# Operands of VectorE in PSUM, one scale per weight matrix, lo in one piece, and two evacuations by either engine

## The chip, the core and the metric

The kernel runs on one core of a Trainium2 chip. The core has a matrix engine (TensorE, PE in the views; its weight loads are the row PEld), VectorE (DVE), ScalarE (ACT), GpSimd (POOL) and SyncE (SP), which here only starts DMAs. The engines work side by side; each goes through its own queue in order and waits on semaphores for the others. SBUF is the memory of 128 partitions that all of them work in; PSUM holds eight banks of 512 fp32 columns, into which TensorE writes. The metric is the device time of one execution in microseconds. Inputs are laid out by the host before the launch and the output is put in order after it; neither is in the time.

## What is computed

Attention with normalised queries and keys (8 batches, 12 heads, 448 tokens, 64 columns a head), and behind it a two-layer block whose input is a mixture of each token with the one before:

```python
def rmsnorm(x, g):
    rms = np.sqrt(np.mean(x * x, axis=-1, keepdims=True) + 1e-06)
    return x / rms * g
q_n, k_n = (rmsnorm(q, g_q), rmsnorm(k, g_k))
scores = scale * np.matmul(q_n, k_n.transpose(0, 1, 3, 2))
scores = scores - np.max(scores, axis=-1, keepdims=True)
attn = np.exp(scores)
attn = attn / (np.sum(attn, axis=-1, keepdims=True) + 1e-09)
x = np.matmul(attn, v)            # heads side by side: 8 x 448 x 768
x_prev = x shifted by one token, the first one zero
xk = mu_k * x + (1.0 - mu_k) * x_prev
xr = mu_r * x + (1.0 - mu_r) * x_prev
k = np.maximum(xk @ w_k, 0.0)     # 768 x 1024
v = k * k @ w_v                   # 1024 x 768
r = 1.0 / (1.0 + np.exp(-(xr @ w_r)))   # 768 x 768
out = r * v
```

q, k and v are fp32; the three weight matrices come as 64-bit floats. Products are made in fp16 with each operand split in two, hi and lo (lo is what rounding to hi leaves over), as hi x hi + hi x lo + lo x hi, and for the first three quads in fp32.

## The kernel before

A *quad* is four heads of a batch (24 quads `u`), a *pair* is two of them (48). For each quad `stats` sums squares and takes the inverse root by three Newton steps on 28 columns (`rsqrt`, line 425; tiles `sst`, `stm`, `ss`), `preps` scales q and k and brings them into transposed form (`stk`). `scores` goes through seven *groups* a quad (168 in all): the products of 128 query rows with all keys, for two heads, into two PSUM banks. `expo` takes the row maximum (VectorE) and the exponential with its sum (ScalarE). `probs` and `split` divide by the sum and write hi (ScalarE) and lo (VectorE, two instructions: columns 384 to 447 first, then 0 to 383, into a tile `nat` in which lo is turned by 64 columns), which a DMA transpose carries to `pT`; 21 groups, those of the first three quads, go through `probs_pe` instead, with transposes on TensorE. `attends` multiplies a pair with v and ScalarE evacuates the result into `x`. `vprep` makes v's scale, hi (ScalarE) and lo (VectorE) for the pairs from 6 on.

`mix` makes xk and xr of a batch, twice six pieces of 448 columns: GpSimd scales the previous token into `df`, VectorE adds the scaled token, ScalarE writes hi and GpSimd lo. `moe` multiplies: first xk with w_k in eight pieces (`square`: ScalarE relu into `kf`, ScalarE square for hi, GpSimd square and lo), then for each 128 tokens xr with w_r and kk with w_v, by halves of 384 columns (`gate`: three ScalarE tanh of 128 columns with a scale each; `store`: VectorE product, GpSimd scaling by columns, DMA out).

The weights come in 20 tiles of 128 columns (8 of w_k, 6 of w_r, 6 of w_v), each in two halves. `wload` starts the DMAs on ScalarE's queue, in rows of 1 KB, into `raw`. `weights` makes fp32 of the 64-bit values (GpSimd the low bits, ScalarE the high ones into PSUM, VectorE puts them together in `wf`). `wsplit` makes a scale for each tile: the diagonal of its Gram matrix on TensorE, taken out with `dg`, summed over partitions, the maximum in `WSC`; then hi and lo, for tiles 1 to 13 by GpSimd scaling, ScalarE cast and GpSimd subtraction, for the others by ScalarE and VectorE. The first half of a batch in `moe` needs all of w_k, the second half needs all 20 tiles (`wdone == NW`).

The order of instructions on every engine is written out when the program is made: each of these functions is a thread that yields instructions, and `Plan.run` emits next the one that can start first by the planner's own clocks, with a bonus for priority. `price` says how long an operation takes, `held` models that VectorE and GpSimd block each other, `wprio` raises the weights' priority when they lag behind one tile per `W_GAP` (10 us). PSUM banks are handed out by `Share`: scores up to five and never the last free one, products (and the weights' high bits) two, `ot` two.

## Time and profile before

| | before |
|---|---|
| median of 3 runs (lowest, highest) | 1018.15 us (1014.79, 1019.3) |
| the profiled execution | 1015.21 us, span of its instructions 1013.4 us |
| granted TensorE clock, mean | 0.961 |
| TensorE busy | 926.0 us (91%) |
| VectorE busy | 812.7 us (80%) |
| ScalarE busy | 746.0 us (74%) |
| GpSimd busy | 691.8 us (68%) |
| DMA queue of SP (q1), of ScalarE (q10) | 129.20 MB, 57.0% of 16 engines; 17.77 MB, 5.9% |

The profile is one execution seen by the hardware profiler. Almost all instructions carry one line number, that of the planner's call, so groups are told apart by operation and tile names: `out<-in`, buffer numbers left out. Tile names ending in x (`natx`, `dfx`) are further buffers of the same kind, and some early tiles lie in space lent by `kk` and `xk` and carry that name. Busy time is the union of an engine's instructions; a busy TensorE need not be at its peak, as matmuls overlap.

### The profile page before, as it was taken

What the parts mean: (1) busy time and instruction counts of PE and PEld (TensorE: products, weight loads), DVE (VectorE), ACT (ScalarE), POOL (GpSimd) and SP (SyncE); (2) the same over time, 40 slices, a digit from 0 to 9 for tenths busy, and PEclk for the clock granted to TensorE, in tenths of its full rate; (3) what the DMA queues carried; (4) which work ended last, traced back from release to release, by engine and by line L of the source; (5) the groups of instructions that cost most, each with busy time, mean ns of one, the idle gap of its engine ahead of it and who ended that gap; (6) DMA issues with size and microseconds to landing.
All of it is one profiled execution on the core that took longest, in us unless ns stands there. A gap on an engine that the chain in (4) does not pass through costs nothing. (4 is left out here: it accounts for less than half of the span.)

```text
span 1013.4 us, 18593 instructions
## 1 busy us (share of the span) xinstructions
PE 926.0 (91%) x6082; PEld 485.8 (48%) x6082; DVE 812.7 (80%) x2260; ACT 746.0 (74%) x1756; POOL 691.8 (68%) x734
## 2 busy tenths in 40 slices
PE   2588869669999999999999999899999999999998
PEld 2354434335544555455545555355545454455564
DVE  5879998999998698979997998799997989763000
ACT  3667878878788789888887887878886988952311
POOL 2787889743798747877886859855987478556501
PEclk9878979869999999999999999999999999999999
DMA  7322349667788789569847977869858884640000
GB/s 248 119 80 86 118 120 221 170 166 169 172 165 168 143 197 203 133 152 201 207 105 173 214 158 161 161 131 201 175 126 177 186 183 110 146 107 32 1 32 32
DMA packets 371138, 148.17 MB, mean 146 GB/s; under 512 B 338272, under 2 KB 355168, under 8 KB 371040
## 3 DMA queue, kind: packets, MB, share of 16 engines
q1 hardware_dynamic: 351792, 129.20, 57.0%
q10 hardware_dynamic: 19248, 17.77, 5.9%
q8 instruction: 48, 0.79, 0.3%
q14 instruction: 50, 0.41, 0.1%
HBM read 51.98 MB, written 11.01 MB: 62 GB/s over the span
## 5 line engine op out<-in xcount | busy, mean ns | idle before, releaser
L273 PE MATMUL ps<-wvh,kk 128*128 128x384 f16 x896 | 233.1, 326 | 0.8 <-DVE nat L273 0.8
L273 ACT ACTIVATE ps<-ps,sums 128x448 f32<-128x448 f32 x294 | 181.9, 621 | 52.5 <-DVE sums L273 48.9
L273 PE MATMUL ps<-xk,wkh 128*128 128x448 f16 x768 | 210.5, 356 | 4.8 <-DVE wf L273 3.9
L273 DVE SCALAR_TENSOR_TENSOR nat<-ps,sums,nat 128x64 f16<-128x64 f32 x480 | 190.7, 439 | 19.2 <-ACT nat L273 17.8
L273 DVE TENSOR_REDUCE sums<-ps 128x1 f32<-128x448 f32 x336 | 193.7, 612 | 15.4 <-PE ps L273 15.1
L273 PE MATMUL ps<-wrh,xr 128*128 128x384 f16 x672 | 179.9, 331 | 2.1 <-DVE nat L273 2.0
L273 ACT ACTIVATE nat<-ps,sums 128x448 f16<-128x448 f32 (+1 forms) x272 | 167.8, 659 | 16.9 <-DVE sums L273 7.1
L273 PEld LDWEIGHTS <-kk 128*128 128x128 f16 (+1 forms) x1362 | 129.2, 98 | 98.7 <-issue 13.5
L273 PE MATMUL ps<-stk 64*128 64x448 f16 (+3 forms) x1104 | 134.2, 390 | 26.4 <-ACT xk L273 6.2
L273 PE MATMUL ps<-wvl,kk 128*128 128x384 f16 x448 | 146.0, 326 | 0.0
L273 PE MATMUL ps<-xk,wkl 128*128 128x448 f16 x384 | 136.5, 355 | 0.0
L273 PEld LDWEIGHTS <-xr 128*128 128x128 f16 x1008 | 96.4, 99 | 80.1 <-issue 16.9
L273 PE MATMUL ps<-wrl,xr 128*128 128x384 f16 x336 | 111.1, 331 | 0.0
L273 PEld LDWEIGHTS <-wkh 128*128 128x128 f16 x768 | 71.9, 99 | 81.6 <-issue 21.6
L273 POOL TENSOR_TENSOR o<-o,bsc 128x384 f32<-128x384 f32 x48 | 43.3, 902 | 88.3 <-DVE o L273 52.3
L273 DVE SCALAR_TENSOR_TENSOR o<-o,ps 128x384 f32<-128x384 f32 x56 | 30.5, 545 | 87.7 <-PE ps L273 59.2
L273 PE MATMUL ps<-pT,vh 128*64 128x448 f16 x588 | 93.8, 363 | 1.4 <-DMA pT<-nat 0.7
L273 ACT ACTIVATE o<-ps,bsc 128x128 f32<-128x128 f32 x144 | 45.6, 387 | 51.2 <-PE ps L273 33.1
L273 POOL TENSOR_TENSOR qk<-qk,ss 128x896 f32<-128x896 f32 x36 | 64.0, 1778 | 22.1 <-DVE ss L273 14.9
L273 PEld LDWEIGHTS <-stk 64*128 64x128 f16 x1008 | 35.0, 98 | 78.0 <-issue 35.5
L273 DVE SCALAR_TENSOR_TENSOR df<-x,bsc,df 128x448 f32<-128x448 f32 x68 | 61.0, 910 | 5.8 <-POOL df L273 5.7
L273 POOL TENSOR_TENSOR nat<-nat 128x448 f32<-128x448 f32 x41 | 48.2, 1175 | 23.6 <-ACT nat L273 17.1
(161 smaller groups left out, 1813.7 us busy)
## 6 DMA issues: line engine op xcount, KB each, us to landing
vf<-in_v_dram SPq DMA_DIRECT2D x48, 256.0 KB, 3.0
out_dram<-o SPq DMA_DIRECT2D x28, 384.0 KB, 2.7
...
```

What stands on the lines that cost most here:

```text
L273: r = op.fn(op.kw["out"], op.kw["value"]) if op.fn.__name__ == "memset" else op.fn(**op.kw)
```

## The change

- **VectorE's operands.** The Newton steps work with the sum and the helper in a PSUM bank; so do v's exponents. In `mix` ScalarE, no longer GpSimd, scales the previous token, into PSUM, and VectorE reads it there. v's hi and lo are made like the GpSimd tiles of the weights (GpSimd, ScalarE, GpSimd). Some small scalings (`probs_pe`, `batch_scales`, `outscale`) go to GpSimd. PSUM shares of their own: `wz` (2) for the weights' high bits, `pg` (1), `df` (2, not the last free bank).
- **lo.** `split` writes lo in one instruction of 448 columns, no longer turned; v comes from the host in 14 blocks in place of 8 (448 KB a pair from pair 6 on), with the rows that lo meets.
- **The weights' scales.** One scale per matrix. A tile is unpacked into the place of the next tile's hi and lo in `WS` (the last one into `wf`); the Gram matrices of all tiles add up in one bank `pg`; `wscale` makes the scale once, and then `wsplit` makes hi and lo tile by tile, each when the one before is done. The even tiles take the GpSimd way. `gate` becomes one tanh of 384 columns, `store` one GpSimd scaling of 768. The loads are started on SP's queue, from a layout in which a tile's half is contiguous in each partition.
- **Either engine.** The relu in `square` and the evacuation in `attends` go to ScalarE or VectorE, whichever the planner's clock has free first.
- **The planner.** New prices, `W_GAP` 7 us, one `wf`, two `df` throughout (before: a third one late).

The core of the diff (the removed lines of weights and wsplit, which stand in the listing above, are left out):

```diff
-WF_BUFS = 2
+WF_BUFS = 1
 PT_BUFS = 2
 STK_BUFS = 2
 X_BUFS = 9
 SC_SHARE = (5, 1)
 MM_SHARE = (2, 0)
 OT_SHARE = (2, 0)
-LOW_TILES = range(0, 20)
-POOL_TILES = range(1, 14)
+WZ_SHARE = (2, 0)
+PG_SHARE = (1, 0)
+DF_SHARE = (2, 1)
+POOL_TILES = range(0, 20, 2)
...
-W_GAP = 10e3
+W_GAP = 7e3
...
-LATE_BUFS = (("kf", 1), ("df", 1), ("nat", 1))
+LATE_BUFS = (("kf", 1), ("nat", 1))
...
+def shares(op):
+    aa = [x for x in op.kw.values() if isinstance(x, bass.AP)]
+    if op.eng == "POOL":
+        return True
+    if any(in_psum(x) for x in aa):
+        return False
+    return op.kw.get("in1") is not None or op.fn.__name__ in FAST
...
     def stats():
...
+            qs = yield from banks["df"].get()
+            sm, tm = qs[:, 0:NSS], qs[:, NSS:2 * NSS]
+            yield V.tensor_scalar(out=sm[:, 0:2 * NT], in0=ss[:, 0:2 * NT], scalar1=1.0 / HD, scalar2=1e-6, op0=ALU.mult, op1=ALU.add)
+            yield V.tensor_scalar(out=sm[:, 2 * NT:NSS], in0=ss[:, 2 * NT:NSS], scalar1=gm[:, 3:4], scalar2=gm[:, 4:5], op0=ALU.mult, op1=ALU.add)
+            yield from rsqrt(V, y, sm, tm)
+            banks["df"].put(qs)
...
     def vprep(js):
...
+            if V_POOL:
+                yield G_.tensor_scalar(out=vf, in0=vf, scalar1=sv, scalar2=0.0, op0=ALU.mult, op1=ALU.add)
+                yield A.copy(out=vh, in_=vf)
+                yield G_.tensor_tensor(out=vl, in0=vf[:, 0:2 * NSL], in1=vh[:, 0:2 * NSL], op=ALU.subtract)
...
     def split(j, sp, r, ph, E):
-        for a, n, o in ((S - HD, HD, S), (0, S - HD, S + HD)):
-            yield V.scalar_tensor_tensor(out=ph[:, j, o:o + n], in0=sp[:, a:a + n], scalar=r[:, j:j + 1], in1=ph[:, j, a:a + n], op0=ALU.mult, op1=ALU.subtract)
+        yield V.scalar_tensor_tensor(out=ph[:, j, S:2 * S], in0=sp[:, 0:S], scalar=r[:, j:j + 1], in1=ph[:, j, 0:S], op0=ALU.mult, op1=ALU.subtract)
...
     def attends():
...
-                yield A.activation(out=x[:, 1 + lo:1 + hi, :].rearrange("p t c -> p (t c)"), in_=av[:, o:o + (hi - lo) * HD], func=AF.Copy, scale=1.0 if iv is None else iv)
+                xo, ao = x[:, 1 + lo:1 + hi, :].rearrange("p t c -> p (t c)"), av[:, o:o + (hi - lo) * HD]
+                if plan.pick("ACT", "DVE") == "ACT":
+                    yield A.activation(out=xo, in_=ao, func=AF.Copy, scale=1.0 if iv is None else iv)
+                else:
+                    yield V.tensor_scalar(out=xo, in0=ao, scalar1=1.0 if iv is None else iv, scalar2=None, op0=ALU.mult)
...
     def mix(b, d, which, dst, df, cnt):
...
-        yield G_.tensor_scalar(out=df, in0=xp, scalar1=sc[:, j + ND:j + ND + 1], scalar2=0.0, op0=ALU.mult, op1=ALU.add)
-        yield V.scalar_tensor_tensor(out=df, in0=xc, scalar=sc[:, j:j + 1], in1=df, op0=ALU.mult, op1=ALU.add)
+        pb = yield from banks["df"].get()
+        yield A.activation(out=pb[:, 0:S], in_=xp, func=AF.Copy, scale=sc[:, j + ND:j + ND + 1])
+        yield V.scalar_tensor_tensor(out=df, in0=xc, scalar=sc[:, j:j + 1], in1=pb[:, 0:S], op0=ALU.mult, op1=ALU.add)
+        banks["df"].put(pb)
...
     def wload():
...
-                yield A.dma_start(out=raw[:, 0:hk, :], in_=w[i * P:(i + hk) * P, c * P:(c + 1) * P].bitcast(I32).rearrange("(i p) n -> p i n", p=P))
-                RAW[ci, i] = raw
+                yield SP.dma_start(out=raw[:, 0:2 * hk * P], in_=w[c, h].bitcast(I32))
+                RAW[ci, h] = raw
...
     def weights():
         for nm, w, kt, c, ci in WT:
+            if c == 0:
+                pg = yield from banks["pg"].get()
+            last = ci + 1 in (NF, NF + ND, NW)
+            nb = 2 if ci < NF else 1
+            if last:
+                wf = yield from R["wf"].get(ci < NF)
+                f = wf.rearrange("p i n -> p (i n)")[:, 0:kt * P]
+                WFT[nm] = wf
+            else:
+                f = WS[nm][:, c + 1].rearrange("p a i n -> p (a i n)").bitcast(F32)
             fi = f.bitcast(I32)
+            for h in range(2):
+                yield from until(lambda: (ci, h) in RAW and st["tq"] >= GATE_W)
+                raw = RAW.pop((ci, h))
+                n = kt * P // 2
+                cols = slice(h * n, (h + 1) * n)
+                zb = yield from banks["wz"].get()
+                z = zb[:, 0:n]
+                yield G_.tensor_scalar(out=fi[:, cols], in0=raw.bitcast(mybir.dt.uint8)[:, 0:8 * n].rearrange("p (n b) -> p n b", b=8)[:, :, 3], scalar1=-15.5, scalar2=2.0 ** -5, op0=ALU.add, op1=ALU.mult)
+                yield A.activation(out=z, in_=raw[:, 0:2 * n].rearrange("p (n two) -> p n two", two=2)[:, :, 1].bitcast(F32), func=AF.Prelu, scale=F64_EXP, alpha=F64_NEG)
+                yield V.scalar_tensor_tensor(out=fi[:, cols], in0=z.bitcast(I32), scalar=3, in1=fi[:, cols], op0=ALU.logical_shift_left, op1=ALU.bitwise_or)
+                banks["wz"].put(zb)
                 R["raw"].put(raw)
+            w16 = f.bitcast(BF16).rearrange("p (i n two) -> p i n two", two=2, n=P)[:, :, :, 1]
+            yield [T.matmul(form=("w", 110 * kt), out=pg[:, c % nb * P:(c % nb + 1) * P], lhsT=w16[:, i, :], rhs=w16[:, i, :], start=(c == 0 and i == 0), stop=(last and i == kt - 1)) for i in range(kt)]
+            if last:
+                plan.spawn(wscale(nm, kt, ci - c, ci + 1, pg, nb * P), wprio)
...
+    def wscale(nm, kt, c0, c1, pg, w):
+        sc = WSC[:, c0:c0 + 1]
         sci = sc.bitcast(I32)
+        dg = small.tile([P, 2 * P], F32, name="dg", bufs=1)[:, 0:w]
+        yield V.tensor_tensor(out=dg.rearrange("p (b n) -> p b n", n=P), in0=pg[:, 0:w].rearrange("p (b n) -> p b n", n=P), in1=bcast(ident[:, :], w // P), op=ALU.mult)
+        yield T.matmul(form=("f", 200 + 1.7 * w), out=pg[:, 0:w], lhsT=ones.broadcast_to([P, P]), rhs=dg, start=True, stop=True)
+        yield V.tensor_reduce(out=sc, in_=pg[:, 0:w], axis=AX.X, op=ALU.max)
+        banks["pg"].put(pg)
         yield V.tensor_scalar(out=sci, in0=sci, scalar1=24, scalar2=23, op0=ALU.logical_shift_right, op1=ALU.logical_shift_left)
         yield V.tensor_scalar(out=sci, in0=sci, scalar1=-1.0, scalar2=float(204 << 23), op0=ALU.mult, op1=ALU.add)
+        yield V.tensor_copy(out=WSC[:, c0 + 1:c1], in_=sc.broadcast_to([P, c1 - c0 - 1]))
+        for ci in range(c0, c1):
+            plan.spawn(wsplit(nm, kt, ci - c0, ci, ci + 1 == c1), wprio)
+
+    def wsplit(nm, kt, c, ci, last):
+        yield from until(lambda: st["wdone"] == ci)
+        sc = WSC[:, ci:ci + 1]
+        f = WFT[nm].rearrange("p i n -> p (i n)")[:, 0:kt * P] if last else WS[nm][:, c + 1].rearrange("p a i n -> p (a i n)").bitcast(F32)
+        hi, lo = (WS[nm][:, c, a].rearrange("p i n -> p (i n)") for a in range(2))
         if ci in POOL_TILES:
             yield G_.tensor_scalar(out=f, in0=f, scalar1=sc, scalar2=0.0, op0=ALU.mult, op1=ALU.add)
+            yield A.copy(out=hi, in_=f)
+            yield G_.tensor_tensor(out=lo, in0=f, in1=hi, op=ALU.subtract)
         else:
+            yield A.activation(out=hi, in_=f, func=AF.Copy, scale=sc)
+            yield V.scalar_tensor_tensor(out=lo, in0=f, scalar=sc, in1=hi, op0=ALU.mult, op1=ALU.subtract)
+        if last:
+            R["wf"].put(WFT.pop(nm))
         st["wdone"] += 1
...
     def square(f, z, kk, off, KF):
...
-        yield A.activation(out=kf, in_=z[:, 0:S], func=AF.Relu, scale=RSC[:, f:f + 1])
+        if plan.pick("ACT", "DVE") == "ACT":
+            yield A.activation(out=kf, in_=z[:, 0:S], func=AF.Relu, scale=RSC[:, f:f + 1])
+        else:
+            yield V.tensor_scalar(out=kf, in0=z[:, 0:S], scalar1=RSC[:, f:f + 1], scalar2=0.0, op0=ALU.mult, op1=ALU.max)
...
     def gate(h, zr, th, rsu, TH):
-        for c in range(3):
-            m = 3 * h + c
-            yield A.activation(out=th[:, c * P:(c + 1) * P], in_=zr[:, c * P:(c + 1) * P], func=AF.Tanh, scale=rsu[:, m:m + 1])
+        yield A.activation(out=th, in_=zr[:, 0:NH], func=AF.Tanh, scale=rsu[:, 0:1])
...
     def store(h, zv, th, rsu, o, OC, dst, TH):
...
-        yield G_.tensor_tensor(
-            out=th.rearrange("p (c n) -> p c n", n=P), in0=th.rearrange("p (c n) -> p c n", n=P),
-            in1=spread(rsu[:, ND + 3 * h:ND + 3 * h + 3], P), op=ALU.mult)
         OC[h] = True
         if len(OC) == 2:
+            yield G_.tensor_scalar(out=o, in0=o, scalar1=rsu[:, 1:2], scalar2=0.0, op0=ALU.mult, op1=ALU.add)
```

More of the change, by code (lines that the diff above doesn't have):

```diff
@@ L313, in emit @@
                 self.acc = acc
-            if e == "POOL" or e == "DVE" and not any(in_psum(x) for x in op.kw.values() if isinstance(x, bass.AP)) and width(op.kw["out"]) > 2:
+            if e in self.held and shares(op):
                 for a, b in self.held["DVE" if e == "POOL" else "POOL"]:
@@ L456, in attn_moe_kernel @@
     psum = Ring(ps, [P, 512], F32, "ps", 8, plan)
-    banks = {n: Share(psum, *c) for n, c in (("sc", SC_SHARE), ("mm", MM_SHARE), ("ot", OT_SHARE))}
+    banks = {n: Share(psum, *c) for n, c in (("sc", SC_SHARE), ("mm", MM_SHARE), ("ot", OT_SHARE), ("wz", WZ_SHARE), ("pg", PG_SHARE), ("df", DF_SHARE))}
     ident16 = const.tile([P, P], BF16, name="ident16")
@@ L521, in attn_moe_kernel @@
         "wf": Ring(stage, [P, NF, P], F32, "wf", WF_BUFS, plan),
[L522 removed]
+        "raw": Ring(stage, [P, NF * P], I32, "raw", RAW_BUFS, plan),
     }
@@ L572, in mu_stats @@
     def mu_stats():
-        yield from until(lambda: st["lu"] >= 1 and len(WFT))
+        yield from until(lambda: st["lu"] >= 1 and len(RAW))
         yield A.dma_start(out=mu[:, 0, 0, :], in_=mu_k.rearrange("(t p) -> p t", p=P))
@@ L613, in stats @@
             ss = small.tile([P, NSS], F32, name="sst", bufs=3)
-            tm = small.tile([P, NSS], F32, name="stm", bufs=3)
             for n, t in enumerate(LD[u]):
@@ L758, in vprep @@
         if hp + n == NP:
-            if not half:
-                yield inverse(s_[:, NP:2 * NP], s_[:, 0:NP])
             yield from batch_scales(b)
@@ L1011, in inverse @@
     def inverse(o, i):
         return V.tensor_scalar(out=o.bitcast(I32), in0=i.bitcast(I32), scalar1=-1.0, scalar2=float(0x7F000000), op0=ALU.mult, op1=ALU.add)
-    def wsplit(nm, kt, c, ci, f):
-        cs = slice(c * P, (c + 1) * P)
-        wh, wl = WS[nm]
-        f = f[:, 0:kt, :]
-        w16 = f.bitcast(BF16).rearrange("p i (n two) -> p i n two", two=2)[:, :, :, 1]
-        pg = yield from banks[WB(ci)].get()
-        yield [T.matmul(form=("w", 110 * kt), out=pg[:, 0:P], lhsT=w16[:, i, :], rhs=w16[:, i, :], start=(i == 0), stop=(i == kt - 1)) for i in range(kt)]
-        sc = WSC[:, ci:ci + 1]
-        sci = sc.bitcast(I32)
-        dg = small.tile([P, P], F32, name="dg", bufs=1)
-        yield V.tensor_tensor(out=dg, in0=pg[:, 0:P], in1=ident, op=ALU.mult)
-        yield T.matmul(form=("f", 400), out=pg[:, P:2 * P], lhsT=ones.broadcast_to([P, P]), rhs=dg, start=True, stop=True)
-        yield V.tensor_reduce(out=sc, in_=pg[:, P:2 * P], axis=AX.X, op=ALU.max)
-        banks[WB(ci)].put(pg)
+    def wscale(nm, kt, c0, c1, pg, w):
+        sc = WSC[:, c0:c0 + 1]
+        sci = sc.bitcast(I32)
+        dg = small.tile([P, 2 * P], F32, name="dg", bufs=1)[:, 0:w]
[3 more added lines that the diff above has]
+        banks["pg"].put(pg)
```

153 lines of the change are left out of this document (68 added, 85 removed).

## The prediction

> **What bounds the kernel now.** First the timeline of TensorE, for the ends of the stages (start, length, group of instructions).
>
> ```profile
> 141.01 0.91 PE L273 MATMUL ps<-xk,wkh 128*128 128x448 f16 x2 [3.90 <-DVE wf L273]
> ...
> 186.83 0.35 PE L273 MATMUL ps<-xk,wkl 128*128 128x448 f16 x1
> ...
> 227.46 0.50 PE L273 MATMUL ps<-wrh,xr 128*128 128x384 f16 x1 [1.39 <-DVE nat L273]
> ```
>
> The key products of batch 0 run from 141 to 187 us; its second half (products with wr and wv) starts only at 227. With these bounds, the windows view, one row for each stretch:
>
> ```profile
> core 0: us, PE busy (x) PEld busy (x) DVE busy (x) ACT busy (x) POOL busy (x), PEclk, DMA share, GB/s
> 0.00:50.00 50.00, 20.32 (x105) 13.53 (x107) 35.72 (x113) 25.07 (x51) 24.55 (x32) 0.91 0.56 183
> 50.00:141.00 91.00, 73.22 (x428) 40.24 (x425) 81.98 (x225) 67.56 (x164) 74.83 (x101) 0.86 0.32 98
> 141.00:187.00 46.00, 42.09 (x254) 21.64 (x253) 39.31 (x101) 38.69 (x83) 43.32 (x42) 0.94 0.76 178
> 187.00:227.00 40.00, 24.32 (x149) 11.79 (x148) 36.85 (x108) 30.32 (x62) 21.87 (x25) 0.68 0.75 185
> 227.00:289.00 62.00, 60.88 (x423) 32.42 (x424) 59.93 (x176) 52.12 (x128) 37.78 (x37) 0.96 0.86 176
> 289.00:890.00 601.00, 586.49 (x4005) 298.42 (x4004) 532.54 (x1492) 498.31 (x1190) 442.45 (x448) 0.99 0.75 164
> 890.00:1013.00 123.00, 118.63 (x725) 67.76 (x723) 26.33 (x51) 33.92 (x84) 47.05 (x55) 1.00 0.14 42
> ```
>
> As a rough measure I take TensorE's work in a stretch as its busy time times the granted clock. What it loses is then 31.5 us up to 50, 91 - 73.2 x 0.86 = 28.0 up to 141, 6.4 up to 187, 40 - 24.3 x 0.68 = 23.5 up to 227, 3.6 up to 289, 20.4 in the 601 us after that, and 4.4 at the end. From 227 on the kernel is TensorE's; freeing another engine there can bring little. What can be won lies in 50:141 and 187:227 (51.5 us together), and in both VectorE is the fullest engine (82.0 of 91, 36.9 of 40). Why the second half waits for 227, the tile view of WSC says (shortest/median/longest ns, first to last start):
>
> ```profile
> L273 DVE TENSOR_REDUCE WSC<-ps x20: 272/280/293, 24.4 to 224.4; 128x1 f32<-128x128 f32 x20
> ...
> L273 DVE SCALAR_TENSOR_TENSOR wvl<-wf,WSC,wvh x6: 1276/1389/2156, 177.4 to 227.3; 128x1024 f16<-128x1024 f32 x6
> ```
>
> It waits for the last of 20 weight tiles, whose scale comes at 224.4 and whose lo starts at 227.3. The tiles come (224.4 - 24.4)/19 = 10.5 us apart.
>
> **The change part by part, up to 227.** VectorE's groups in the window 0:228 (busy us, mean ns of one | idle before):
>
> ```profile
> L273 DVE SCALAR_TENSOR_TENSOR nat<-ps,sums,nat 128x384 f16<-128x384 f32 x28 | 16.9, 604 | 0.0
> L273 DVE SCALAR_TENSOR_TENSOR df<-x,bsc,df 128x448 f32<-128x448 f32 x12 | 10.7, 908 | 0.0
> ...
> L273 DVE TENSOR_SCALAR sums<-sums 128x2 f32<-128x2 f32 x21 | 8.9, 426 | 1.3 <-ACT nat L273 1.3
> ...
> L273 DVE SCALAR_TENSOR_TENSOR nat<-ps,sums,nat 128x64 f16<-128x64 f32 x28 | 7.7, 274 | 1.2 <-ACT nat L273 1.0
> ...
> L273 DVE SCALAR_TENSOR_TENSOR stm<-stm,ss 128x28 f32<-128x28 f32 x18 | 6.2, 343 | 0.4
> L273 DVE SCALAR_TENSOR_TENSOR ss<-stm,ss 128x28 f32<-128x28 f32 x18 | 6.1, 337 | 0.4
> L273 DVE TENSOR_SCALAR WSC<-WSC 128x1 int32<-128x1 int32 x40 | 5.8, 144 | 0.2
> ...
> L273 DVE TENSOR_TENSOR dg<-ps,ident 128x128 f32<-128x128 f32 x20 | 5.6, 280 | 0.8 <-PE ps L273 0.8
> ...
> L273 DVE SCALAR_TENSOR_TENSOR vl<-vf,bstat,vh 128x512 f16<-128x512 f32 x5 | 5.0, 1007 | 0.0
> L273 DVE TENSOR_TENSOR stm<-sst,ss 128x28 f32<-128x28 f32 x18 | 4.3, 241 | 0.4
> ...
> L273 DVE TENSOR_SCALAR sums<-ps 128x2 f32<-128x2 f32 x15 | 2.2, 149 | 1.7 <-ACT ps L273 1.7
> ```
>
> And one of them in the tile view of ss, again shortest/median/longest:
>
> ```profile
> L273 DVE SCALAR_TENSOR_TENSOR stm<-stm,ss x18: 177/188/1511, 15.7 to 204.8; 128x28 f32<-128x28 f32 x18
> ```
>
> - Newton steps (stm, ss). The same instruction takes 188 ns in the middle and 1511 at worst, so some of them wait behind another engine; a two-column TENSOR_SCALAR takes 426 ns on average with both ends in SBUF and 149 with a PSUM source. The change puts one operand of each step in PSUM; I price them at 187 (bounds 149 and the means of now): 54 instructions, 16.6 - 10.1 = 6.5 us saved. The four preparing instructions of each quad I count as unchanged.
> - sums<-sums goes to GpSimd: 8.9 saved.
> - One scale per matrix, not per tile: dg, the reduction (20 x 280) and WSC take 17.0 us for 20 tiles; three rounds at up to twice the width, some 1.2 each. Saved 13.4.
> - vl goes to GpSimd: 5.0 saved.
> - df with one operand in PSUM is like the nat rows: their slope is (604 - 274)/320 = 1.03 ns a column, so 604 + 64 x 1.03 = 670 ns; 12 x 0.24 = 2.9 saved (at worst nothing).
> - lo in one instruction of 448 in place of 64 and 384. Busy times overlap, so durations overstate it (274 + 604 - 670 = 208 ns). A run of four of 384 and three of 64 in the timeline, which gives the group its first form's name:
>
> ```profile
> 503.00 2.77 DVE L273 SCALAR_TENSOR_TENSOR nat<-ps,sums,nat 128x384 f16<-128x384 f32 x7
> ```
>
> That is (2.77 - 0.60)/3 = 0.72 us a pair; one of 448 should pace at 0.60. 28 x 0.12 = 3.4 saved (bound 5.8).
>
> Sum for VectorE: 40 of the 193.9 us that the windows give it up to 227.
>
> [...]
>
> GpSimd's and ScalarE's groups in the same window, and two lines of the page on DMA:
>
> ```profile
> L273 POOL TENSOR_SCALAR raw<-raw 128x384 int32<-128x384 uint8 x20 | 12.5, 623 | 5.9 <-DMA raw<-in_moe_w_k_dram 3.7 <-DMA raw<-in_moe_w_r_dram 0.7
> ...
> L273 POOL TENSOR_SCALAR wf<-wf,WSC 128x768 f32<-128x768 f32 x11 | 11.0, 999 | 1.9 <-DVE WSC L273 0.7 <-PE ps L273 0.6
> L273 POOL TENSOR_TENSOR wrl<-wf,wrh 128x768 f16<-128x768 f32 x6 | 9.8, 1641 | 1.5 <-ACT wrh L273 1.4
> L273 POOL TENSOR_SCALAR df<-x,bsc 128x448 f32<-128x448 f32 x12 | 8.4, 710 | 1.1 <-DVE bsc L273 1.0
> ...
> L273 POOL COPY x<-x 128x63 f32<-128x63 f32 x9 | 2.4, 271 | 6.7 <-ACT x L273 6.7
> ```
>
> ```profile
> L273 ACT ACTIVATE kf<-ps,RSC 128x448 f32<-128x448 f32 x8 | 5.1, 633 | 4.5 <-PE ps L273 4.2 <-issue 0.3
> ...
> L273 ACT CAST wrh<-wf 128x768 f16<-128x768 f32 x6 | 5.0, 828 | 0.5 <-issue 0.2 <-POOL wf L273 0.2 <-POOL xk L273 0.2
> ...
> L273 ACT ACTIVATE x<-ps,bstat 128x448 f32<-128x448 f32 x2 | 1.3, 648 | 0.0
> ```
>
> ```profile
> q10 hardware_dynamic: 19248, 17.77, 5.9%
> ...
> vf<-in_v_dram SPq DMA_DIRECT2D x48, 256.0 KB, 3.0
> ```
>
> ScalarE, 161.6 us up to 227: twelve previous-token products like the 648 row, +7.8; five v casts of 896 columns, by the 828 row 0.97 each, where now 512 are cast, +1.5 at most; half of the eight relus handed to VectorE, -2.5. Makes 168; VectorE gets those 2.5 and stands at 156. The 40 weight DMAs leave ScalarE's queue too; issuing is not in its busy time, and I count it as nothing. GpSimd, 164.6: -8.4 for df; v with a scaling of 896 and a subtraction of 512 columns, by the 768 rows 1.17 + 1.09, five times, +11.3; 21 sums of at most 0.27, +5.7; three split tiles fewer at 2.6, -7.9. Makes 165. So the fullest engine falls from 193.9 to 168. If it fills the stretch as well as VectorE does now (193.9/227 = 0.85), batch 0's second half starts at 168/0.85 = 198: **29 us** earlier.
>
> Counted as nothing, with what covers it. Weight loads move to SP's queue and wait there for a free raw buffer; behind them stand the q, k and v loads and the transposes. The cover is a DMA share of 0.32 in 50:141; without it a load lands late by about one landing, 3 us by v's row, a few times. The v cast now waits for GpSimd, with normalisation and squares queued behind it there; the cover is two v buffers, so a pair's product stands a pair away. df now waits for ScalarE, behind exponentials; if that cover goes, a mix costs 0.65 us more in a chain of six. From pair 6 on v grows from 256 to 448 KB: 42 x 0.19 = 8 MB, by queue 10's row 2.7% of the DMA engines, on a share of 0.75. After 227, ScalarE's 84 more products (55 us) lie on 498 of 601, about what VectorE carries now, before what it hands over; VectorE's relief (lo, Newton, df, vl) goes into TensorE's 20.4 lost us, of which I take **4** (bounds 0 and 12). At the end stands one GpSimd step of 768 for one of 384: nothing.
>
> Sum: 1013.4 - 33 = 980 span. The profiled execution took 1015.2, 1.8 more than its span, and the median of the three runs, 1018.15, lies 2.9 above that: **985 us**.
>
> **The rivals.**
> (a) More: of the 51.5 us in 50:141 and 187:227 45 go, and 8 later: 965. For it: VectorE stands at 0.9 in both; against: GpSimd is at 0.82 in the first.
> (b) Order, not load: the stretch up to 227 is set by waits in chains and by eight PSUM banks, not by the fullest engine. Weights now get two banks of their own, the scale holds one throughout, df up to two, where the weights had used those of the products; scores get what is left. Then only the 4 us come: 1014. For it: ScalarE and GpSimd stay at 0.71 to 0.74 of the stretch. That the relus and evacuations stay on ScalarE after all would cost 2.5 us of busy time here and falls under this.
> (c) Slower: the splits of a matrix can no longer go tile by tile as they come. All of it must be unpacked before its scale is known, and tile c is written where the raw values of tile c-1 lay, so the splits follow one another. For wv a GpSimd tile is 999 + 828 + 1641 ns at 768 columns, 4.6 us at 1024; a VectorE tile 828 x 4/3 + 1389 = 2.5; three of each, 21 us after the last scale, where now 3 follow. If unpacking keeps its 10.5 us a tile, the second half starts 18 us later: 1018 + 18 - 4 = 1032. It decides from (200 - 18)/19 = 9.6 us a tile. For it: the chain is in the code. Against: one unpacking takes 623 ns of GpSimd, two make a tile, so the 10.5 us are a pace that the planner holds (W_GAP), and the change sets it to 7.
>
> **How the numbers follow.** Forecast (974 to 998) 0.48, (a) 0.20, (b) (1006 to 1021) 0.16, (c) 0.16. A measurement of this kernel can tell about 0.5%, 5 us, from no change. Faster: the forecast, (a) and 0.06 of (b), 0.74; same 0.10; slower (c), 0.16. The range runs from 952 (a quarter of (a) lies below) to 1028 (some 0.10 of (c) above).
>
> **What would show it.** Right: the first product with wr before 205; VectorE near 156 us busy in 0:227; Newton steps under 200 ns on average, none over 1000; a 448-column lo near 670. Wrong: the first product with wr after 220, behind the last wv split (c), or, with no engine over 0.75 up to there, behind PSUM banks (b); and TensorE under 0.97 busy in the long middle would mean that the 4 us are a loss.

## The result, and the profile after

| | before | after |
|---|---|---|
| median of 6 runs (lowest, highest) | 1017.03 us (1014.79, 1019.3) | 1009.44 us (1008.8, 1013.52) |
| ratio, 95% interval | | 0.9932 [0.991, 0.9954] |
| span of the profiled execution | 1013.4 us | 1007.0 us |

Medians are of fast executions throughout; one slow execution of the version p1 below (2383 us) is left out.

The change gains 0.7%, where 3.2% were forecast. First the page of the changed kernel, the rows of busy time and of SyncE's DMA queue:

```profile
PE 913.7 (91%) x6048; PEld 479.1 (48%) x6048; DVE 702.1 (70%) x1887; ACT 741.0 (74%) x1648; POOL 677.6 (67%) x765
...
q1 hardware_dynamic: 357552, 154.76, 70.5%
```

VectorE has lost 110.6 us of busy time (812.7 to 702.1), and TensorE some 12 (926.0 to 913.7), which the prediction had not counted. The windows with the bounds of the prediction's first table (same columns):

```profile
core 0: us, PE busy (x) PEld busy (x) DVE busy (x) ACT busy (x) POOL busy (x), PEclk, DMA share, GB/s
0.00:50.00 50.00, 19.25 (x92) 12.63 (x92) 27.02 (x92) 19.39 (x41) 17.87 (x31) 0.90 0.52 171
50.00:141.00 91.00, 68.48 (x419) 36.83 (x417) 71.49 (x185) 68.39 (x158) 76.36 (x114) 0.92 0.49 154
141.00:187.00 46.00, 22.78 (x128) 11.38 (x129) 35.60 (x85) 36.90 (x74) 32.39 (x32) 0.59 0.58 151
187.00:227.00 40.00, 39.06 (x256) 19.27 (x255) 31.96 (x85) 36.51 (x82) 32.52 (x38) 1.00 0.54 109
227.00:289.00 62.00, 61.40 (x441) 31.95 (x440) 53.61 (x153) 56.35 (x129) 46.27 (x51) 1.00 1.04 211
289.00:890.00 601.00, 590.71 (x4055) 302.07 (x4054) 466.08 (x1266) 505.24 (x1137) 443.19 (x470) 1.00 0.88 177
```

The hole in TensorE's work that lay at 187:227 is closed, and another has opened in front of it: 22.8 busy us of the 46 in 141:187. The timeline of TensorE shows what moved (start, length, group):

```profile
177.66 1.30 PE L289 MATMUL ps<-stk 64*128 64x448 f16 x6 [5.02 <-DVE nat L289]
...
186.20 1.11 PE L289 MATMUL ps<-xk,wk 128*128 128x448 f16 x5
```

```profile
226.29 3.10 PE L289 MATMUL ps<-wr,xr 128*128 128x384 f16 x18
```

The key products of batch 0 start at 186 in place of 141 (8 us before, TensorE stood 5.0 us for a tile of VectorE's), the second half at 226 in place of 227.5. From here on I read TensorE's idle time (stretch less its busy time) instead of landmarks, since other products can fill the time before a landmark. Up to 300 us and behind it, before and then after:

```profile
0.00:300.00 300.00, 231.84 (x1421) 124.81 (x1422) 264.73 (x745) 222.59 (x505) 213.22 (x245) 0.88 0.61 155
300.00:1013.40 713.40, 694.12 (x4662) 360.99 (x4660) 547.93 (x1516) 523.39 (x1252) 478.62 (x490) 1.00 0.64 143
```

```profile
0.00:300.00 300.00, 221.97 (x1397) 117.17 (x1399) 229.49 (x618) 228.26 (x502) 215.47 (x272) 0.90 0.65 164
300.00:1007.00 707.00, 691.77 (x4653) 361.93 (x4649) 472.59 (x1270) 512.77 (x1147) 462.10 (x494) 1.00 0.74 151
```

Up to 300 TensorE idles 300 - 221.97 = 78.0 us, 9.9 **more** than before (68.2), although VectorE has 35 us less to do there. Behind 300 it idles 15.2, 4.1 less than before (19.3). With the 12.2 us that it no longer works by these windows: 9.9 - 4.1 - 12.2 = -6.4, which is the change of the span. One thing that TensorE was spared is plain in its groups, before and then after:

```profile
L273 PE MATMUL ps<-dg,ones 128*128 128x128 f32 x40 | 11.0, 365 | 4.7 <-DVE dg L273 4.6
```

```profile
L289 PE MATMUL ps<-dg,ones 128*128 128x128 f32 x4 | 1.0, 326 | 0.0
L289 PE MATMUL ps<-dg,ones 128*128 128x256 f32 x2 | 0.7, 430 | 0.0
```

One scale per matrix takes 34 fp32 products off TensorE: 11.0 us of them become 1.7, 9.3 us less. All of them lay before 225 us, where TensorE idles much, so these 9.3 us need not be as much in time. The first cause of the longer idle time stands in the waits of the first 30 us, TensorE's and VectorE's, and in the DMAs there (KB each, us from issue to landing):

```profile
PE ps L289 <- DVE mucol L289: 8.3, 1, 8.3
```

```profile
DVE mu L289 <- DMA mu<-in_moe_mu_r_dram: 6.1, 1, 6.1
```

```profile
mu<-in_moe_mu_k_dram ACTq DMA_DIRECT2D x1, 3.0 KB, 10.9
mu<-in_moe_mu_r_dram ACTq DMA_DIRECT2D x1, 3.0 KB, 11.9
```

In `mu_stats` one word has changed: the loads of mu start when a raw weight tile has been asked for (`len(RAW)`), not when the first is unpacked (`len(WFT)`). They are now issued at 5.6 and 6.0 us, in place of 14.9 and 20.8, and land after 10.9 and 11.9 us (3.7 and 4.8 before); VectorE's first step on mu starts at 18.0 in place of 41.2. VectorE stands for them, in order, until 18, TensorE behind VectorE, and the first transposes come at 23.7 in place of 18.7.

### The profile page after: what moved, and what is told of

Same layout as the page of the kernel before. It is cut to its first block, busy times and chain, and to the rows that moved or that the text cites. A ratio compares the mean times of both kernels' runs of the same rounds, so it can differ in the third digit from the quotient of the medians.

```text
span 1007.0 us, 18155 instructions
## 1 busy us (share of the span) xinstructions
PE 913.7 (91%) x6048; PEld 479.1 (48%) x6048; DVE 702.1 (70%) x1887; ACT 741.0 (74%) x1648; POOL 677.6 (67%) x765
## 5 line engine op out<-in xcount | busy, mean ns | idle before, releaser
L289 PE MATMUL ps<-wv,kk 128*128 128x384 f16 x1344 | 234.8, 326 | 0.0
L289 PE MATMUL ps<-xk,wk 128*128 128x448 f16 x1152 | 226.6, 353 | 0.0
L289 DVE TENSOR_REDUCE sums<-ps 128x1 f32<-128x448 f32 x336 | 192.1, 614 | 21.7 <-PE ps L289 20.8
L289 PE MATMUL ps<-wr,xr 128*128 128x384 f16 x1008 | 176.6, 326 | 4.0 <-DVE bstat L289 2.7
L289 DVE SCALAR_TENSOR_TENSOR nat<-ps,sums,nat 128x448 f16<-128x448 f32 x238 | 156.3, 676 | 29.7 <-ACT nat L289 27.4
L289 PEld LDWEIGHTS <-wk 128*128 128x128 f16 (+1 forms) x1194 | 113.2, 99 | 113.0 <-issue 15.6
L289 PEld LDWEIGHTS <-xr 128*128 128x128 f16 x1008 | 96.0, 98 | 75.4 <-issue 10.9
L289 DVE SCALAR_TENSOR_TENSOR df<-x,bsc,ps 128x448 f32<-128x448 f32 x96 | 63.5, 673 | 23.0 <-ACT ps L289 18.0
L289 POOL TENSOR_TENSOR xr<-df,xr 128x448 f16<-128x448 f32 x48 | 49.2, 1038 | 36.0 <-ACT xr L289 35.0
L289 POOL TENSOR_SCALAR o<-o,bsc 128x768 f32<-128x768 f32 x24 | 21.8, 910 | 76.6 <-DVE o L289 60.5
L289 POOL TENSOR_TENSOR nat<-qk,nat 128x896 f16<-128x896 f32 x31 | 58.6, 1891 | 11.7 <-ACT nat L289 11.7
L289 POOL TENSOR_SCALAR vf<-vf,bstat 128x896 f32<-128x896 f32 x42 | 42.7, 1017 | 31.5 <-ACT ps L289 14.2
L289 POOL TENSOR_TENSOR xk<-df,xk 128x448 f16<-128x448 f32 x48 | 49.8, 1039 | 20.4 <-ACT xk L289 18.5
```

The costliest lines, as they stand in the source:

```text
L289: r = op.fn(op.kw["out"], op.kw["value"]) if op.fn.__name__ == "memset" else op.fn(**op.kw)
```

## The experiments

Each kernel was timed beside the kernel before on the same chips; ratios are to that kernel, with their 95% interval. Idle times are TensorE's, up to 300 us and behind it; TensorE's, VectorE's and GpSimd's busy times are those of the whole span; all are from the one profiled execution. Idle times and TensorE's busy time add up to its span.

| kernel | median us | ratio | idle to 300 | idle after | TensorE | VectorE | GpSimd |
|---|---|---|---|---|---|---|---|
| before |  | 1 | 68.2 | 19.3 | 926.0 | 812.7 | 691.8 |
| after | 1009.44 | 0.9932 [0.991, 0.9954] | 78.0 | 15.2 | 913.7 | 702.1 | 677.6 |
| e1 | 999.46 | 0.9847 [0.9826, 0.9867] | 66.2 | 16.3 | 915.2 | 704.4 | 678.4 |
| e2 | 1017.2 | 1.0018 [1.0004, 1.0032] | 78.5 | 16.3 | 919.3 | 703.7 | 680.5 |
| e3 | 997.53 | 0.9832 [0.9809, 0.9855] | 66.9 | 19.2 | 909.4 | 705.3 | 680.6 |
| e4 | 1018.17 | 1.0024 [1.001, 1.0039] | 70.4 | 23.6 | 921.6 | 661.0 | 680.6 |
| f1 | 1019.68 | 1.0045 [1.0033, 1.0058] | 79.4 | 21.7 | 917.7 | 735.2 | 677.2 |
| f2 | 1053.1 | 1.0379 [1.0356, 1.0401] | 87.6 | 38.5 | 926.1 | 749.4 | 677.9 |
| n1 | 1006.02 | 0.9898 [0.9873, 0.9923] | 72.0 | 22.1 | 911.9 | 730.0 | 678.6 |
| p1 | 1029.01 | 1.0142 [1.0123, 1.016] | 78.2 | 24.1 | 924.2 | 815.6 | 688.8 |
| p2 | 1020.86 | 1.0049 [1.0032, 1.0066] | 73.3 | 24.4 | 919.5 | 788.9 | 688.8 |
| p3 | 1025.59 | 1.0082 [1.0057, 1.0106] | 73.3 | 26.3 | 925.4 | 773.4 | 604.6 |
| g1 | 999.0 | 0.9841 [0.9827, 0.9854] | 69.9 | 17.0 | 910.0 | 784.1 | 680.0 |
| w1 | 996.88 | 0.9803 [0.977, 0.9837] | 65.6 | 16.5 | 913.5 | 703.2 | 680.5 |
| w2 | 998.0 | 0.9816 [0.9792, 0.9841] | 60.5 | 19.7 | 915.4 | 699.4 | 680.1 |
| s1 | 1004.26 | 0.9887 [0.9868, 0.9907] | 72.4 | 14.6 | 913.2 | 783.3 | 600.7 |
| s2 | 1002.1 | 0.9872 [0.9852, 0.9892] | 61.5 | 23.0 | 916.5 | 713.1 | 656.4 |
| s3 | 1000.89 | 0.9857 [0.9841, 0.9874] | 64.7 | 19.7 | 915.1 | 704.1 | 681.3 |
| s4 | 1031.43 | 1.0154 [1.0129, 1.0178] | 77.4 | 36.5 | 915.7 | 726.4 | 761.2 |
| s5 | 1001.01 | 0.9839 [0.9812, 0.9866] | 66.0 | 17.7 | 916.0 | 741.4 | 602.6 |

Any edit makes the planner write a new order for the whole kernel, except in f1 and f2, which keep the changed kernel's. I take differences of up to some 4 us between such versions for chance of the order; that is an assumption, drawn from the many edits that gave 997 to 1001. TensorE's busy time is no constant of its products either: the changed kernel's 6048 products take from 909.4 (e3) to 926.1 us (f2). The granted clock may be part of it (mean 0.976 in e3, 0.955 in f2), but e4's 921.6 us come at 0.966 and the changed kernel's 913.7 at 0.967; no run here shows why.

### mu's loads (e1, p1)

e1: the changed kernel with the instructions on mu held until the first quad's transposed keys are done; the two loads are still issued early (at 6.3 and 6.7 us).

```diff
+        yield from until(lambda: st["tq"] >= 1)
         yield V.tensor_scalar(out=mu[:, :, 1, :], in0=mu[:, :, 0, :], scalar1=-1.0, ...
```

> Changed kernel, with the instructions on mu held back until the first quad is prepared. Theory (part of the loss is VectorE standing 6.1 us before 18 us for mu's load, everything queued behind): TensorE's first transposes come at 19 us in place of 23.7, batch 1's key products 4 to 5 us earlier than 287, time 1004 to 1006. Rival (the stop is made up for later, since no engine is full up to 187): transposes at 19, batch 1's key products still at 285 to 289, time 1007 to 1011.

999.46 us: 0.9% faster than the changed kernel (0.9847 against 0.9932, intervals apart), below both ranges. The idle time up to 300 falls by 11.8, to 66.2, two below that of before; behind 300 it rises by 1.1. The first transposes come at 19.1 again; the gain is more than the theory said. Only 2.8 of the 11.8 us lie in the first 30 us; how the stop there grows to the rest was not taken apart.

p1 does the reverse, in the kernel before:

```diff
-        yield from until(lambda: st["lu"] >= 1 and len(WFT))
+        yield from until(lambda: st["lu"] >= 1 and len(RAW))
```

> The kernel before, with one condition of the changed one: the two loads of mu start as soon as a raw weight tile is loading, not when the first one is unpacked. Theory (VectorE's stop for mu is a cost of its own that came with the change): VectorE stands for mu for 5 us or more before 20 us, TensorE's first transposes come at 23 to 24 us in place of 18.7, batch 1's key products start 4 to 10 us later than 288, and the time is 1021 to 1027 us. Rival (the stop matters only with the change's weight loads on the other queue): 1013 to 1020 us.

1029.01 us, 1.4% slower, with 10.0 us more idle up to 300 and the first transposes at 23.2. So mu's early place costs 9 to 14 us of time in either kernel, and 10 to 12 of idle time up to 300. The size was above the range, and the place was not the one the theory named. ScalarE's waits in p1, first 30 us:

```profile
ACT xk L273 <- DMA mu<-in_moe_mu_k_dram: 9.0, 1, 9.0
```

Here the engine put down as standing for mu is ScalarE, with the first quad's squares behind the wait, and VectorE and GpSimd stand behind ScalarE.

### The weights' pace and priority (e2, e3, w1, w2)

e2 is the changed kernel with `W_GAP` 10 us as before; the other three are e1 with `W_GAP` 8 and `PRIO_W` 0 (e3), `PRIO_W` 0 alone (w1), `W_GAP` 8 alone (w2).

```diff
-PRIO_W = 200
+PRIO_W = 0
-W_GAP = 7e3
+W_GAP = 8e3
```

> Changed kernel with the planner's pace for weights put back from 7 to 10 us a tile, nothing else. Theory (the order spends VectorE's relief on weights): batch 0's key products start at 150 to 165 (186 in the changed kernel, 141 before), the last weight tile's hi at 205 to 220 (185, 226 before), batch 1's key products again at 283 to 293: the hole only moves, time 1005 to 1015. Rival (PSUM banks held by weights, scale and df throttle the scores): the key products stay later than 178, whatever the pace.

> Changed kernel with mu held back as in e1, weights at 8 us a tile and their constant priority 200 taken to 0: order alone, the same instructions. Theory (load was relieved, order wasted it): batch 0's key products at 145 to 158, last weight tile's hi at 185 to 205, batch 1's key products at 268 to 277, time 992 to 1000. Rival (the stretch is set by banks or chains, not by the choice between weights and attention): batch 1's key products not before 282, time over 1003.

> The version with mu late (999.5 us), with only the weights' standing priority at 0 in place of 200 and W_GAP still 7. Beside it the version with mu late and W_GAP 8 alone. The version with both gave 997.5 us, with batch 1's key products at 267 in place of 280. Theory (priority of weights over mixes is what holds batch 0's key products back): batch 0's key products start at 150 to 160 in place of 171, batch 1's at 265 to 273, and the time is 992 to 998 us. Rival (the order found by the planner differs by chance): no shift of the key products that goes with either setting, 997 to 1004 us.

> The version with mu late (999.5 us), with only W_GAP at 8 us in place of 7 and the weights' priority still 200. Theory (a wider gap lets the mixes of batch 0 go first): batch 0's key products start at 155 to 165 in place of 171, batch 1's at 270 to 276, and the time is 994 to 999 us. Rival (by chance): 997 to 1004 us.

The slower pace alone costs 8 us (e2), more than its range allowed: the weights' hurry was not the loss. Its key products come at 166, as the theory had it roughly, but batch 1's only at 301; of the 7.1 us by which its span is longer, 1.6 are idle time, the rest is busy time of TensorE. With mu late, batch 0's key products start at 171 (e1), 151 (e3), 158 (w1), 154 (w2), batch 1's at 281, 268, 272, 267, and the last matmuls end at 993, 991, 991, 991. Both settings move the landmarks as far as the theory said or further, and the end hardly: 2 to 3 us, within what a new order does by chance. **w1, 996.9 us, is the fastest version measured**, 2.0% below the kernel before; e3 and w2 cannot be told from it.

### The parts undone in the changed kernel (f1, f2, n1, e4)

f1 writes lo in two instructions again, f2 keeps Newton's sum and helper in SBUF; in both the planner still reckons with the changed form (`op`), and only what is emitted differs (`op.real`), so that the order stays. n1 is f2 with a planner that knows. f1:

```diff
+        op.real = [V.scalar_tensor_tensor(out=ph[:, j, S + a:S + a + n], in0=sp[:, a:a + n], scalar=r[:, j:j + 1], in1=ph[:, j, a:a + n], op0=ALU.mult, op1=ALU.subtract).kw for a, n in ((S - HD, HD), (0, S - HD))]
```

n1 (in f2 the same operands, through `op.real`):

```diff
-            qs = yield from banks["df"].get()
-            sm, tm = qs[:, 0:NSS], qs[:, NSS:2 * NSS]
+            sm = ss
+            tm = small.tile([P, NSS], F32, name="stm", bufs=3)
```

> The changed kernel, with every instruction in the same order, but lo again in two instructions on VectorE (columns 384 to 447, then 0 to 383), as before the change. The prediction's step says a pair paces at 0.72 us and one instruction at 0.60, so VectorE gets about 270 x 0.12 = 32 us more work over the whole run. Theory (VectorE is not what the long middle waits for): the time stays within 0.5% of the changed kernel, 1005 to 1014 us, and VectorE's busy time rises from 702 to 730 or more. Rival (VectorE's lo stands in the chain from scores to probabilities and is felt in the middle): 1015 to 1022 us.

VectorE's busy time rises by 33.1 us over 294 lo, 0.11 us each (the prediction's term: 0.12). The time rises by 1.1%; of 11.8 us of span 6.5 are idle time behind 300, 1.4 up to it and 4.0 busy time of TensorE. The rival was right that lo is felt there when the order is held fixed.

> The changed kernel, with every instruction in the same order, but the Newton steps' sum and helper again in SBUF, as before the change. By the prediction's step the shared-operand waits come back: some of the 216 instructions of a run (three steps of three on 24 quads) take over 1000 ns beside GpSimd's work, the mean goes from about 190 to 300 or more, and VectorE's busy time rises by 15 to 25 us. Theory (the middle does not wait for VectorE, the first three quads do a little): 1008 to 1014 us. Rival (the Newton chain holds up the first quads, so the waits add up at the front): 1016 to 1022 us. [...]

> The changed kernel with the Newton steps' sum and helper in SBUF, as in f2, but with the order of all instructions made anew by a planner that knows of these operands (in f2 it kept the order made for PSUM and lost 44 us). Theory (what f2 lost is a fixed order in which 21 small instructions in a row come out twice as long; a planner that knows of them starts GpSimd's work beside other instructions): 1010 to 1025 us, with a mean Newton step of 200 to 300 ns. Rival (the steps in SBUF cost 1.8 us a quad whatever the order): 1045 to 1055 us.

f2 loses 44 us (3.8% above the kernel before), n1 nothing: 1006.0, below its range, and if anything a little faster than the changed kernel. The steps themselves are as slow in n1 as in f2. One group of the three, for after, f2 and n1 (busy us, mean ns):

```profile
L289 DVE SCALAR_TENSOR_TENSOR ps<-ps,ss 128x28 f32<-128x28 f32 x72 | 13.8, 192 | 1.7
```

```profile
L290 DVE SCALAR_TENSOR_TENSOR stm<-stm,ss 128x28 f32<-128x28 f32 x72 | 21.7, 301 | 1.8
```

```profile
L289 DVE SCALAR_TENSOR_TENSOR stm<-stm,ss 128x28 f32<-128x28 f32 x72 | 21.2, 294 | 1.0
```

So 44 us was not the price of slow steps but of an order written for quicker steps. How, I can only argue: a burst of 13 small instructions comes out late, and all that was to follow it on VectorE waits. (n1 also leaves the `df` bank free that f2's planner still reserves; s3 speaks against a large effect of that, as fewer banks for `df` and `wz` gained nothing there.) The expectation of f2 asked for 1008 to 1014 or, at the front, 1016 to 1022; neither saw this. VectorE stood at 71% in that run.

> Changed kernel with the relus and the value evacuations all on ScalarE again. Theory (no engine is the bound up to 187, TensorE after): within 4 us of the changed kernel's 1009, ScalarE 20 to 35 us more busy. Rival (ScalarE is the new bound and the choice of engine is what brought the 7 us): 1014 to 1022.

```diff
-                if plan.pick("ACT", "DVE") == "ACT":
+                if True:
```

(the same in `square`). 1018.17 us, in the rival's range: the choice of engine is worth 0.9%, about 9 us. It does not show as idle time: that only moves, 7.6 less up to 300 (70.4) and 8.4 more behind it (23.6 against 15.2). TensorE's busy time is 7.9 us longer (921.6) with the same products; why, no run shows.

### hi by either engine (g1)

e3, with hi of the probabilities handed out as relu is:

```diff
-        yield A.activation(out=ph[:, j, 0:S], in_=sp[:, 0:S], func=AF.Copy, scale=r[:, j:j + 1])
+        if plan.pick("ACT", "DVE") == "ACT":
+            yield A.activation(out=ph[:, j, 0:S], in_=sp[:, 0:S], func=AF.Copy, scale=r[:, j:j + 1])
+        else:
+            yield V.tensor_scalar(out=ph[:, j, 0:S], in0=sp[:, 0:S], scalar1=r[:, j:j + 1], scalar2=None, op0=ALU.mult)
```

> The version with mu late, W_GAP 8 and no extra priority for the weights (997.5 us), in which hi of the probabilities, too, is written by ScalarE or VectorE, whichever the planner's clock has free first. Theory (since VectorE was relieved, ScalarE is the engine that the long middle waits for): ScalarE's busy time falls by 30 to 60 us, the time from batch 1's key products to the end falls from 723 to 710 to 718 us, and the whole comes to 985 to 994 us. Rival (ScalarE's hand-over only moves the wait to VectorE, where hi now stands ahead of other steps): 995 to 1004 us.

ScalarE went from 742.6 to 668.2 us, VectorE from 705.3 to 784.1, and the time stayed (999.0 against 997.5). The rival's range is met: ScalarE alone was not what counted.

### One part alone in the kernel before (p2, p3)

p2: Newton's sum and helper in a PSUM bank of their own (a share of one, not the last free one), with the lines of `stats` from the change. p3: the mixes' previous token scaled by ScalarE into such a bank:

```diff
-        yield G_.tensor_scalar(out=df, in0=xp, scalar1=sc[:, j + ND:j + ND + 1], scalar2=0.0, op0=ALU.mult, op1=ALU.add)
-        yield V.scalar_tensor_tensor(out=df, in0=xc, scalar=sc[:, j:j + 1], in1=df, op0=ALU.mult, op1=ALU.add)
+        pb = yield from banks["df"].get()
+        yield A.activation(out=pb[:, 0:S], in_=xp, func=AF.Copy, scale=sc[:, j + ND:j + ND + 1])
+        yield V.scalar_tensor_tensor(out=df, in0=xc, scalar=sc[:, j:j + 1], in1=pb[:, 0:S], op0=ALU.mult, op1=ALU.add)
+        banks["df"].put(pb)
```

> The kernel before with only the Newton steps' sum and helper in a PSUM bank (one bank at a time, never the last free one), order made anew. Theory (this part is worth about 6.5 us of VectorE's time up to the second half of batch 0 and nothing later, since TensorE is busy for 705 of the last 720 us): 1008 to 1014 us. Rival (the part carries the gain of the whole change, as f2 seems to say): 975 to 1000 us. A second rival, the bank that scores no longer have: 1018 to 1025 us.

> The kernel before with only the mixes of the changed one: ScalarE scales the previous token into a PSUM bank (one bank, never the last free one), VectorE adds the other token from there. Theory (df beside GpSimd is a cost of its own: VectorE's step falls from 910 ns to 670 and GpSimd loses 96 steps): 985 to 1005 us. Rival (GpSimd at 68% has room for df as long as v's work does not lie there too; the 34 us of s4 are the two together): 1010 to 1022 us.

Both are slower than the kernel before, by 0.5% and 0.8%, though VectorE loses 23.8 and 39.3 us of work; TensorE idles 5 to 7 us more on either side of 300. p2 is at its second rival, a bank less for scores, though that was not taken apart from the rest. p3 missed both ranges.

### Load, split chain, banks, mixes (s1 to s5), each against w1

s1 takes three reliefs of VectorE back at once (Newton in SBUF, lo in two, v's hi and lo by ScalarE and VectorE), s5 only the last. s2 leaves no weight split to GpSimd. s3 gives one PSUM bank each to `wz` and `df`. s4 lets GpSimd scale the previous token into SBUF again.

The edits of s2 and s3; in s1 and s5 `V_POOL` is False, s1 has the lines of f1 (planned as such) and n1 besides, and s4 is p3's diff turned round:

```diff
-POOL_TILES = range(0, 20, 2)
+POOL_TILES = range(0)
```

```diff
-WZ_SHARE = (2, 0)
+WZ_SHARE = (1, 0)
-DF_SHARE = (2, 1)
+DF_SHARE = (1, 1)
```

> The version with mu late and the weights' standing priority at 0 (996.9 us), with three of VectorE's reliefs taken back together and the order made anew: Newton's sum and helper in SBUF, lo in two instructions, v's hi and lo by ScalarE and VectorE. VectorE's busy time goes from 703 to about 780. Theory (order, not load, sets the stretch up to 300; TensorE's own work sets the rest): TensorE idles up to 300 us within 6 us of the 65.6 it idles there now, and the time is 994 to 1005 us. Rival (the load of the fullest engine sets the stretch, as the prediction had it): 20 us more idle up to 300, 1014 to 1025 us.

> The version of 996.9 us with all 20 weight splits by ScalarE and VectorE (2.5 us a tile by the prediction's rows) in place of every second one by GpSimd (4.6 us). Theory of the prediction's rival (c) (the splits in series are what the second half of batch 0 waits for): the last hi comes 5 to 8 us earlier than 178, and the time is 988 to 993 us. Rival (the chain is covered by the products with w_k): 995 to 1000 us.

> The version of 996.9 us with one PSUM bank in place of two for the weights' high bits and one in place of two for df and Newton, so that up to two more banks are free for scores. Theory (banks set the stretch up to 300): TensorE idles 8 to 15 us less there, and the time is 982 to 990 us. Rival (banks are not what is short; the weights and mixes lose a buffer): 995 to 1004 us.

> The version of 996.9 us with the mixes as before the change: GpSimd scales the previous token into SBUF, VectorE adds the other one there. ScalarE's busy time falls by about 55 us, GpSimd's rises by 60. Theory (the three engines are about equally full up to 300, and VectorE then waits for GpSimd beside it): 1000 to 1012 us. Rival (ScalarE's 7.8 us up to 227 and 55 later are what ate the relief): 985 to 993 us.

> The version of 996.9 us with v's hi and lo as in the kernel before (ScalarE casts with the scale, VectorE subtracts), the rest unchanged. GpSimd's busy time falls from 681 to about 600, VectorE's rises from 703 to about 745. Theory (no engine but TensorE is short, and s1's 7 us came from Newton and lo): 993 to 999 us. Rival (VectorE's order suffers from 42 more steps of 1 us): 1000 to 1006 us.

s1 is the test of the prediction's main step. The windows up to 300 and behind it of w1, and then of s1:

```profile
0.00:300.00 300.00, 234.39 (x1464) 119.76 (x1465) 242.34 (x631) 238.69 (x526) 227.48 (x280) 0.91 0.68 169
300.00:995.60 695.60, 679.11 (x4586) 356.58 (x4583) 460.90 (x1251) 505.97 (x1127) 453.01 (x486) 1.00 0.73 152
```

```profile
0.00:300.00 300.00, 227.56 (x1436) 118.38 (x1437) 258.91 (x708) 235.43 (x518) 199.93 (x255) 0.88 0.67 167
300.00:1000.30 700.30, 685.67 (x4614) 359.34 (x4611) 524.44 (x1506) 519.42 (x1141) 400.79 (x427) 1.00 0.74 152
```

80 us of VectorE's relief are worth 7.4 us (0.8% by the ratios, 0.9887 against 0.9803), and 6.8 us of idle time up to 300, for 16.6 us of VectorE's work there; behind 300, where it carries 63.5 more, TensorE idles no longer than before. The theory's range of time is met, its bound of 6 us by a little not; the rival asked for 20. s5's 4 us are within chance. Neither s2 nor s3 gains: with no split left to GpSimd the last hi still comes at 177 (178 in w1), and with other banks the idle time up to 300 is 64.7 for 65.6. s3's time is in its rival's range; s2 is 5 us slower than w1, 2 above its rival's range. s4 loses 34 us, far above both ranges. VectorE's step in the mixes in w1 and in s4:

```profile
L289 DVE SCALAR_TENSOR_TENSOR df<-x,bsc,ps 128x448 f32<-128x448 f32 x96 | 63.8, 674 | 23.2 <-ACT ps L289 17.2 <-POOL xr L289 4.1 <-POOL xk L289 1.2
```

```profile
L289 DVE SCALAR_TENSOR_TENSOR df<-x,bsc,df 128x448 f32<-128x448 f32 x96 | 101.4, 1064 | 18.8 <-POOL df L289 18.5 <-POOL x L289 0.2
```

674 ns become 1064 (910 in the kernel before), and GpSimd, which has v's work now, stands at 761 us. So v's work on GpSimd needs the mixes' scaling off it. The reverse does not hold: s5 has the mixes on ScalarE without v on GpSimd, and loses nothing clear. Why the same move loses 0.8% in the kernel before (p3) stays open.

## Why the prediction was wrong, and where it was right

**The step that failed** is "If it fills the stretch as well as VectorE does now (193.9/227 = 0.85), batch 0's second half starts at 198", and with it that the 29 us of an earlier start are 29 us of time. The load came out near the forecast. The window of the changed kernel up to 227:

```profile
0.00:227.00 227.00, 149.57 (x891) 80.11 (x892) 166.08 (x444) 161.19 (x352) 159.13 (x213) 0.86 0.52 149
```

The fullest engine has 166.1 us there (forecast 168), though it is VectorE, for which 156 were forecast; ScalarE has 161.2 (168), GpSimd 159.1 (165). But the fullest engine fills 0.73 of the stretch, not 0.85: the fill was not a property of the stretch. Less work only made VectorE idler.

That the start of the second half is no measure of the time, w1 shows. It starts at 196.5 there, as forecast, and VectorE has 155.4 us up to then (forecast 156). Up to the second half, the kernel before and then w1:

```profile
0.00:227.00 227.00, 159.96 (x933) 87.20 (x933) 193.87 (x544) 161.64 (x358) 164.56 (x197) 0.85 0.54 148
0.00:196.50 196.50, 138.24 (x811) 71.98 (x812) 155.38 (x395) 145.92 (x316) 151.67 (x199) 0.89 0.54 155
```

The start lies 31.0 us earlier, but TensorE has been busy 21.7 us less by then; some 9 of them are the products with `dg`, which are gone. From there to the end w1 takes 799.1 us, 13.2 more than the kernel before (785.9), and TensorE is busy there for 9.3 us more: work was put off. So 31.0 us of an earlier start are 17.8 of span. Against e1, where the second half starts at 217.8, 21 us of earlier start go with 2.6 us of time.

TensorE's idle time up to 300 does not follow VectorE's load there: 68.2 us go with 264.7 of VectorE in the kernel before, 78.0 with 229.5 after, 72.4 with 258.9 in s1, 65.6 with 242.3 in w1. The direct figures are 6.8 us of idle time for 16.6 of load (s1 against w1), and in n1 a stretch that idles 6.0 less with 18.8 more. So load counts for something, far less than the forecast had it.

**What was in its place**, for the stretch up to 300: mu's early steps, which wait for its loads, some 12 us of idle time (e1; p1 gives 10 in the other kernel). The prediction does not mention them, though the line is in the whole diff: of the moved steps I had counted the weight DMAs alone. With these steps late the stretch idles 66.2 us (e1), 2 less than before. So **rival (b)**, order more than load, is what happened. That its range, 1006 to 1021, holds the measured time is in part luck, as it did not name mu either. That it is the eight banks, as (b) also had it, s3 doesn't bear out. What does set the remaining 66 us is open. Some 21 of them lie in the first 30 us. Changed one at a time, the split chain (s2), the banks (s3), the weights' priority (w1) and their pace (w2) moved the sum by 6 us at most, VectorE's load by 7 (s1).

**Rival (c)** was right in its price and wrong in its weight. The splits run in series, and one kind is dearer than thought. The tile view of wv on VectorE (shortest/median/longest ns, first and last start):

```profile
L289 DVE SCALAR_TENSOR_TENSOR wv<-wv,WSC x2: 2068/2230/2392, 172.2 to 179.3; 128x1024 f16<-128x1024 f32 x2
L289 DVE SCALAR_TENSOR_TENSOR wv<-wf,WSC,wv x1: 1284/1284/1284, 186.6 to 186.6; 128x1024 f16<-128x1024 f32 x1
```

The two long steps start at 172.23 and 179.29, while GpSimd is in an instruction that ends at 173.23 and at 180.61; each ends 1.07 us after that. From 165 to 188 wv's six tiles take 23 us (priced at 21). But the unpacking ended at 156, faster than the 9.6 us a tile from which (c) decides, so the chain ended beside the late key products.

**The long middle** came out as forecast: 4 us, and 4.1 measured as idle time behind 300. The agreement of the number is luck as much as anything, as that idle time goes from 14.6 to 19.7 us among s1, w1, e3 and w2. But TensorE was busy for 694 of 713 us there already, and that bounds what any other engine's relief can bring.

**A term that was missing**: TensorE's own work, 12.2 us less, 9.3 of them the products with `dg`. The prediction took the work around them off VectorE and nothing off TensorE. By the idle times alone the change would have lost 5.8 us. What the term is worth in time is not shown: the products lay where TensorE idles, and p2, with all products of the kernel before, has 6.5 us less of busy time and is no faster.

**Prices.** Newton steps: forecast 187, measured 183 to 192, none over 196 (up to 1583 before). lo of 448 columns: forecast 670, measured 676. df: 670, measured 673. v's cast: 0.97, measured 965 ns. The hand-over to VectorE, "2.5 us" up to 227, was read there alone; over the whole run it is 9 us of time (e4). The cover for v's 8 MB, a share of 0.75, went: 289:890 has 0.88. What that costs was not tried alone.

The median of a Newton step is 186 to 195 ns with operands in PSUM (after), 186 to 188 in SBUF (n1, f2); the longest takes 196 ns with operands in PSUM (after), 1890 (n1) and 1920 (f2) in SBUF. In the kernel before the two longest, of 1511 and 1583 ns, start at 62.19 and 91.76 us while GpSimd is in an instruction that ends at 63.66 and at 93.30; each ends 0.04 us after that.

**Which part brings the gain** is only half settled. The choice of engine brings 9 us (e4), lo some in the order as it stands (f1; by f2 and n1 that need not be its price in an order made anew), mu costs 9 (e1). Newton's PSUM operands bring nothing once the order is made anew (n1), and cost 0.5% alone (p2). One scale per matrix, the contiguous weight loads and the planner's new prices were not tried alone; there is no run that isolates TensorE's 12.2 us.
